# A fused attention, routing and MLP kernel on one core: a new order of the attention, fewer key transfers, one bank for the slots, earlier gathers

## The chip, the core and the metric

The kernel runs on one core of one Trainium2 chip. The time is the device time of one execution in microseconds (us). The core's engines work side by side, each through its own list of instructions in program order: PE multiplies matrices (its weight loads, PEld, overlap), DVE and ACT and POOL work on vectors, SP issues transfers. Matmul results stand in PSUM, eight banks; the other data in SBUF. An instruction that waits holds up all that stand behind it on its engine.

## What is computed

Three stages in a row on 4 batches of 768 tokens, width 384.

```python
# 1: linear attention, 8 heads of 48, complex decay a (|a| clipped at 0.999)
for t in range(768):
    S_re, S_im = ar * S_re - ai * S_im + k_t (x) v_t, ar * S_im + ai * S_re
    y[t] = q_t @ S_re
# 2: mixture of experts: a token with x @ w_skip > 0 goes to its best of 8 experts
e = argmax(x @ w_gate); out = x + prob[e] * relu(x @ w1[e]) @ w2[e]   # w1: 384 x 1024
# 3: dense MLP
h = x @ w_in; out = (h * sigmoid(h)) @ w_out                          # w_in: 384 x 2048
```

## The kernel before

**Attention.** The 768 tokens are six chunks of 128, and the batches two pairs; the pair of a chunk and a batch pair is a step, 12 in all (s = 0 to 11). For each step the kernel loads a, k, q and v; takes the logarithm of the magnitude and the angle of a (`clip`, `ln`, `exp`, `z`, `sq`, `ln1p`, `atan`); sums both over the chunk by matmuls with triangular matrices (L309: `lsc`, `lpu`, `lpy`, `run` for the log sums, `rpy`, `rpu`, `rpx`, `rtp`, `run` for the angles); takes exponentials, sine and cosine; and multiplies k and q by them (`kc`, `qc` with the cosine, `ksn`, `qsn` with the sine, all L243, into the tiles `o`). Steps 0 and 1 do this in two halves, one batch each (`CUTS`).

The result `o`, with real and imaginary parts in two tiles C and S, must be laid out anew, channel by channel, as `KQ`. Transfers from SBUF to SBUF do this (L446, one per row of `PIECES`, five for each of C and S and half). PE then transposes the keys (`tp`, L472), takes scores (`sc`, L482), masks them (`P`, on DVE), multiplies by the values (`py`, L500, and by the state, L504), forms the update of the state (`pu`, L515), and turns the result (`yT`) back into rows of tokens (`px`, L532), which are copied (`xr`) and stored (L541).

**Routing.** After each chunk the logits are taken (`lg` in the table, `pl` on PE, L575), flipped by a small matmul (L584) and copied (`lgo`, L590). From them DVE makes the best expert, the rank of each token within its expert, and a one-hot matrix; matmuls (L835) turn these into slots, 256 tokens for each expert: token numbers (`slots[0]`, read at L858 to L866) and gates (`slots[1]`). The last chunk has its own part (`r1...`), the rest is `r0...`. Each kind of slot has a PSUM tile of its own.

**Order.** Attention and routing are not scheduled by the compiler: `PLACE` gives each piece of each step a position (two values for the two halves), `TAIL` each piece of the routing, and `at` sorts them. Each engine's list is in that order. `ENG` says which engine does a piece (V is DVE, G is POOL, A is ACT). The queues are in the same order: SP issues loads, key transfers and stores one behind the other, POOL the indirect transfers.

**Experts.** Of each expert's 256 tokens POOL gathers two tiles of 128 rows (L989); PE turns them (`pt`, L1001; `xh` is ACT's rounded copy, L1059), multiplies up (`ph`, L925 and L935), ReLU, down (`py`, L935); DVE applies the gates (L1045), POOL scatters the rows back (L1049). A scatter waits for the one before it, since they write the same buffer. Where gathered tokens are late, small matmuls on ones keep PE going (L982). The order comes here from times: `start(e)` is 16.35 x e - 6, and `at(start(e & 6) - 28 + ...)` places the gathers of experts 4 to 7, both experts of a pair at the same time.

**Dense MLP.** Six groups of 512 tokens; POOL gathers the first groups' rows back (`xr`, L1339), PE turns them (`pt`, L1347), multiplies up, ACT and DVE do the SiLU, PE multiplies down, and the result is stored.

Of the kernel before, what the change touches and what calls it, by code (L numbers as in the profile page):

```python
# [8 lines left out]
F32 = mybir.dt.float32  # L9
# [15 lines left out]
W = 2 * H * D  # L25
# [4 lines left out]
DP = 64  # L30
# [9 lines left out]
    "ldA": (0, 5, 10, 40, 85, 48, 103, 261, 306, 336, 397, 494),  # L40
    "clip": ((1, 2), (15, 14), 20, 61, 153, 159, 278, 281, 368, 386, 451, 542),
# [6 lines left out]
    "expc": ((28, 27), (106, 87), 113, 182, 242, 307, 356, 427, 486, 530, 595, 659),  # L48
    "stt2": ((37, 38), (109, 97), 118, 190, 250, 321, 375, 450, 491, 540, 622, 685),
    "cumL": ((39, 42), (115, 104), 138, 208, 266, 343, 391, 453, 525, 554, 625, 689),  # L50
    "expE": ((47, 50), (124, 112), 170, 228, 273, 347, 416, 485, 550, 565, 645, 723),
    "expI": ((53, 83), (123, 120), 162, 220, 280, 350, 414, 478, 537, 567, 653, 714),
    "atan": ((12, 18), (56, 66), 68, 147, 209, 268, 324, 392, 454, 511, 590, 691),
    "cumA": ((16, 34), (59, 72), 93, 176, 234, 288, 362, 426, 499, 583, 656, 732),
    "tn1": ((17, 44), (75, 77), 114, 194, 253, 309, 372, 429, 506, 586, 662, 743),
    "wrap": ((29, 45), (89, 91), 126, 198, 254, 313, 380, 434, 517, 592, 663, 746),
    "car": (67, 111, 141, 236, 272, 326, 418, 484, 526, 599, 0, 0),
    "carl": (73, 116, 142, 247, 312, 328, 439, 497, 552, 606, 0, 0),
    "abs": ((33, 65), (125, 102), 149, 248, 297, 319, 398, 441, 524, 597, 679, 761),
    "sin": ((78, 82), (144, 133), 201, 256, 333, 365, 448, 507, 557, 639, 702, 762),  # L60
    "cos": ((62, 69), (129, 139), 193, 252, 341, 371, 436, 508, 564, 627, 680, 778),
    "ldK": (19, 35, 130, 187, 279, 299, 389, 474, 513, 580, 665, 700),
# [6 lines left out]
    "ksn": ((88, 107), (154, 184), 206, 270, 335, 423, 463, 546, 626, 670, 720, 770),  # L69
    "qsn": ((80, 95), (155, 177), 219, 269, 360, 405, 498, 527, 609, 649, 706, 782),  # L70
    "dmaC": ((100, 128), (164, 213), 257, 295, 366, 417, 496, 573, 650, 696, 763, 804),
    "dmaS": ((101, 110), (178, 207), 239, 285, 385, 440, 509, 566, 652, 697, 750, 792),
    "ldV": (76, 71, 55, 339, 340, 455, 492, 549, 655, 614, 767, 755),
# [31 lines left out]
    "flip": (0, 323, 0, 443, 0, 581, 0, 671, 0, 803, 0, 839),  # L105
    "lgb": (0, 344, 0, 462, 0, 632, 0, 677, 0, 805, 0, 841),
    "lgo": (0, 352, 0, 465, 0, 637, 0, 682, 0, 811, 0, 842),
}
TAIL = {
# [41 lines left out]
def consts(tc, k):  # L151
# [36 lines left out]
    (0, 48, 2, 0, 3, 0, 0),  # L188
    (1, 48, 2, 0, 3, 3, 0),
    (96, 32, 1, 0, 2, 6, 0),  # L190
    (96, 16, 1, 2, 1, 6, 32),
    (112, 16, 1, 2, 1, 7, 32),
)

# [1573 lines left out]
```

## Time and profile before

| what | us |
|---|---|
| three runs | 780.03, 777.7, 779.22 |
| median | 779.22 |
| profiled execution | 778.55 |
| its span (first to last instruction) | 776.8 |
| PE busy | 744.7 (96%), 5499 matmuls |
| DVE busy | 535.4 (69%) |
| ACT busy | 438.2 (56%) |
| POOL busy | 207.4 (27%) |
| mean granted clock of PE | 0.993 of full speed |

The span is 1.75 us shorter than the execution. The attention lasts to about 218 us in the trace, the experts to about 362, the dense MLP to the end. The busy share is a mean over these stages; where PE is idle, and for what it waits, stands in the rows below.

### The profile page before, as it was taken

Reading aid. Unit: us, or ns where it says so; the run is one execution under the profiler, and the core shown is the slowest. Engines: PE = TensorE matmul, PEld = TensorE weight load, DVE = VectorE, ACT = ScalarE, POOL = GpSimd, SP = SyncE. Lnnn points to the kernel's source line nnn. Section 1 sums busy time; section 2 is a strip of 40 time slices with the busy share of each in tenths; the row PEclk is TensorE's granted clock in tenths of the full one; section 3 lists DMA queues with packets and bytes.
Section 4 is the critical chain, followed back from the end, with each engine's and each line's share of the span. In section 5 each row is a group of like instructions: output and inputs, shape, how many; then the busy total and the mean of one; then the engine's idle time right before and its main releaser. Section 6 shows DMA issues by size and latency. Waiting matters only on the chain.

```text
span 776.8 us, 13952 instructions
## 1 busy us (share of the span) xinstructions
PE 744.7 (96%) x5499; PEld 686.8 (88%) x5499; DVE 535.4 (69%) x957; ACT 438.2 (56%) x718; POOL 207.4 (27%) x193
## 2 busy tenths in 40 slices
PE   2799999999999999999999999999999999999995
PEld 2799999998889999999999998988888888888885
DVE  6899889999755867669898333654565656556544
ACT  7899889955435545455676212344555455555543
POOL 4478567123523122423300036810000000000000
PEclk9899999999999999999999999999999999999999
DMA  8567786577838965656760011001000101101001
GB/s 344 166 194 222 267 267 227 164 225 227 276 110 277 304 240 165 248 194 225 228 213 35 1 41 41 1 31 42 12 29 14 42 1 41 41 1 42 1 1 45
DMA packets 31530, 101.87 MB, mean 131 GB/s; under 512 B 4960, under 2 KB 13536, under 8 KB 31456
## 3 DMA queue, kind: packets, MB, share of 16 engines
q1 hardware_dynamic: 26128, 88.05, 34.7%
q0 software_dynamic: 3072, 9.44, 3.3%
q10 hardware_dynamic: 2256, 3.41, 1.4%
q8 instruction: 45, 0.74, 0.4%
q14 instruction: 29, 0.24, 0.1%
HBM read 69.27 MB, written 12.58 MB: 105 GB/s over the span
## 4 chain that ended last, share of the span: by engine, by line
PE 81%; DMA 7%; ACT 4%; DVE 3%; issue 2%; POOL 2%; SPq 1%; another core or an unknown queue 0%; POOLq 0%; DVEq 0%; ACTq 0%
PE ph L935 29%; PE py L935 24%; PE pd L935 6%; PE sc L482 5%; DMA xbuf<-xg,sidx 3%; PE run L309 3%; PE pu L515 2%; PE py L500 2%; PE py L504 2%; PE tp L472 1%; PE ph L925 1%; DMA KQ<-o 1%; PE px L532 1%; DMA xg<-xbuf,gidx 1%; PE pt L1347 1%
## 5 line engine op out<-in xcount | busy, mean ns | idle before, releaser
L935 PE MATMUL ph<-cxh,wh 128*128 128x512 f32 x288 | 113.6, 394 | 0.0
L935 PE MATMUL ph<-cxl,wh 128*128 128x512 f32 x288 | 112.8, 392 | 0.0
L935 PE MATMUL ph<-cxh,wl 128*128 128x512 f32 x288 | 112.6, 391 | 0.0
L1212 DVE TENSOR_TENSOR gl<-g,gh 128x512 fp32r<-128x512 f32 x64 | 44.3, 692 | 88.7 <-ACT gh L1211 45.2
L1210 ACT ACTIVATE g<-ph 128x512 f32<-128x512 f32 x64 | 38.1, 596 | 49.1 <-PE ph L935 48.9
L935 PEld LDWEIGHTS ph<-cxl,wh 128*128 128x128 f32 x288 | 54.0, 188 | 11.6
L935 PEld LDWEIGHTS ph<-cxh,wl 128*128 128x128 f32 x288 | 54.1, 188 | 9.2
L935 PEld LDWEIGHTS ph<-cxh,wh 128*128 128x128 f32 x288 | 54.2, 188 | 9.0
L1232 ACT CAST tz<-twd 128x256 fp32r<-128x256 f32 x96 | 36.6, 408 | 42.5 <-DVE twd L1224 42.5
L1018 DVE TENSOR_TENSOR wl<-raw,wh 128x1536 fp32r<-128x1536 f32 x28 | 48.7, 1758 | 10.7 <-ACT wh L916 10.7
L482 PE MATMUL sc<-KQ 96*128 96x128 f32 x384 | 52.7, 285 | 0.5 <-DMA KQ<-o 0.4
L482 PEld LDWEIGHTS sc<-KQ 96*128 96x128 f32 x384 | 47.8, 197 | 2.7 <-issue 1.4
L935 PE MATMUL ph<-xh,wh 128*128 128x256 f32 x168 | 47.8, 285 | 0.0
L935 PE MATMUL ph<-xl,wh 128*128 128x256 f32 x168 | 47.5, 283 | 0.0
L935 PE MATMUL ph<-xh,wl 128*128 128x256 f32 x168 | 47.5, 283 | 0.0
L916 ACT CAST wh<-raw 128x1536 fp32r<-128x1536 f32 x28 | 40.7, 1478 | 9.0 <-DMA raw<-in_w_dram 7.4
L935 PE MATMUL py<-wh,gl 128*128 128x384 f32 x128 | 43.2, 338 | 0.0
L935 PE MATMUL py<-wh,gh 128*128 128x384 f32 x128 | 43.1, 337 | 0.0
L935 PE MATMUL py<-wl,gh 128*128 128x384 f32 x128 | 43.0, 336 | 0.0
L1049 POOL DMA_INDIRECT xbuf<-xg,sidx x16 | 19.7, 1233 | 86.2 <-DVE xg L1045 24.1
L935 PE MATMUL py<-wh,hh 128*128 128x384 f32 x120 | 40.9, 341 | 0.0
L1211 ACT CAST gh<-g 128x512 fp32r<-128x512 f32 x64 | 39.7, 621 | 2.0
(373 smaller groups left out, 2118.5 us busy)
## 6 DMA issues: line engine op xcount, KB each, us to landing
raw<-in_w_dram SPq DMA_DIRECT2D x30, 768.0 KB
KQ<-o SPq DMA_DIRECT2D x40, 290.2 KB
kq<-in_kq_dram SPq DMA_DIRECT2D x12, 768.0 KB
a<-in_a_dram SPq DMA_DIRECT2D x10, 768.0 KB
raw<-in_w_in_dram SPq DMA_DIRECT2D x8, 768.0 KB
raw<-in_w_out_dram SPq DMA_DIRECT2D x8, 768.0 KB
v<-in_v_dram SPq DMA_DIRECT2D x12, 384.0 KB
xbuf<-xr SPq DMA_DIRECT2D x24, 192.0 KB
```

What stands on the lines that cost most here:

```text
L309: nc.tensor.matmul(p[:, i if bank is None else bank, g * CH:g * CH + CH], a[:, n * CH:n * CH + CH], tri, start=first and g == 0, stop=last ...
L482: nc.tensor.matmul(sc[:, j, :], key(4 * g + j), t.KQ[0:96, 4 * g + j, b, 1, 0:CH], start=True, stop=True)
L500: nc.tensor.matmul(py[64 * i:64 * i + 64, j, :], t.v[:, v0 + h * D:v0 + h * D + DP], u.P[:, h, :], start=True, stop=first)
L504: nc.tensor.matmul(py[64 * i:64 * i + 64, j, :], state[0:96, s0 + h * D:s0 + h * D + DP], t.KQ[0:96, h, b, 1, 0:CH], start=False, stop=True)
L916: nc.scalar.copy(hi, src)
L935: nc.tensor.matmul(out, a, x, start=first and n == 0, stop=last and n == len(pairs) - 1)
L1018: nc.vector.tensor_tensor(u.w[i][1], u.raw[i], u.w[i][0].bitcast(F32), ALU.subtract)
L1049: nc.gpsimd.indirect_dma_start(out=k.x, out_offset=bass.IndirectOffsetOnAxis(ap=k.sidx[:, c:c + 1], axis=0), in_=u.xg[i], in_offset=None)
L1210: nc.scalar.activation(a, u.ph[f], AF.Silu)
L1211: nc.scalar.copy(u.gh[f], a)
L1212: tt(u.gl[f], a, u.gh[f].bitcast(F32), ALU.subtract)
L1232: nc.scalar.copy(h, u.x[:, n])
```

## The change

There are six edits. The numbers of `PLACE`, `TAIL` and `ENG` are new, so attention and routing run in another order and some pieces on another engine. The rows of `PIECES` for the last 16 channels of heads 6 and 7 are interleaved, so three transfers take the place of five. The load of `a` for step 0 comes in four pieces, a half of the tokens' columns each, real and imaginary part, in place of two. The last chunk's rows of the second batch go through the bank `tp`, the other ones through `px`. Both kinds of slots lie in one bank of the tag `pu`; before they had one of `pu` and one of `tp`. The gathers of experts 6 and 7 are placed at the time of expert 5's, 16.35 us earlier in the plan; those of 4 and 5 stay.

Of the tables two lines are shown; the rest of the diff is whole.

```diff
--- before.py
+++ after.py
-    "dmaC": ((100, 128), (164, 213), 257, 295, 366, 417, 496, 573, 650, 696, 763, 804),
...
-    "lg": (0, 302, 0, 431, 0, 575, 0, 669, 0, 790, 0, 837),
...
+    "dmaC": ((103, 136), (175, 202), 238, 302, 364, 425, 494, 577, 619, 682, 748, 789),
...
+    "lg": (0, 308, 0, 446, 0, 588, 0, 663, 0, 805, 0, 835),
...
@@ -188,8 +188,8 @@
     (0, 48, 2, 0, 3, 0, 0),
     (1, 48, 2, 0, 3, 3, 0),
     (96, 32, 1, 0, 2, 6, 0),
-    (96, 16, 1, 2, 1, 6, 32),
-    (112, 16, 1, 2, 1, 7, 32),
+    (96, 16, 2, 2, 1, 6, 32),
+    (97, 16, 2, 2, 1, 7, 32),
 )
 
 
@@ -267,8 +267,9 @@
                 x = pool.tile([128, 2, W], F32, name=n, tag=tag)
                 src = (k.in_a if n == "a" else k.in_kq)[s]
                 if n == "a" and s in CUTS:
-                    for i in range(2):
-                        nc.sync.dma_start(x[:, i], src[:, i])
+                    for sl in CUTS[s] if s == 0 else (slice(0, W),):
+                        for i in range(2):
+                            nc.sync.dma_start(x[:, i, sl], src[:, i, sl])
                 else:
                     nc.sync.dma_start(x, src)
                 if n == "a":
@@ -442,8 +443,9 @@
                 lazy(t, "KQ", lambda: kq[s % len(kq)])
                 b = batches(sl)
                 o = tile(half)[:, :, b]
-                for p0, n, step, g0, ng, h0, d0 in PIECES:
-                    nc.sync.dma_start(t.KQ[every(2 * d0 + half, n, 2), h0:h0 + ng, b], o[every(p0, n, step), g0:g0 + ng])
+                nc.sync.dma_start(t.KQ[every(half, 48, 2), 0:6, b], o[0:96])
+                nc.sync.dma_start(t.KQ[every(half, 32, 2), 6:8, b], o[96:128, 0:2])
+                nc.sync.dma_start(t.KQ[every(64 + half, 16, 2), 6:8, b], o[96:128, 2:3])
 
             for half, x in enumerate("CS"):
                 each(s, "e" + x, lambda i, sl, half=half: ends(half, sl))
@@ -527,7 +529,7 @@
                 tt(sv, tu, dv, ALU.mult)
 
             def rows():
-                px = u.px = ps.tile([128, 4, 2, DP], F32, name="px", tag="px")
+                px = u.px = ps.tile([128, 4, 2, DP], F32, name="px", tag="tp" if last and b else "px")
                 for j in range(4):
                     nc.tensor.transpose(px[:, j].rearrange("p a d -> p (a d)"), t.yT[:, 2 * bp + b, j, :], k.ident)
 
@@ -606,9 +608,10 @@
         end = NSTEP - 1
 
         k.slots = []
-        for tag in ("pu", "tp"):
+        k.bank = None
+        for i in range(2):
             s = Ctx()
-            s.tag, s.tile, s.n = tag, None, 0
+            s.i, s.tile, s.n = i, None, 0
             k.slots.append(s)
 
         def fetch():
@@ -828,7 +831,9 @@
     def fill(g, b, slots):
         m = b.shape[2] * 16
         if slots.tile is None:
-            slots.tile = ps.tile([128, 2, m], F32, name="slots", tag=slots.tag)
+            if k.bank is None:
+                k.bank = ps.tile([128, 2, 2, 48], F32, name="slots", tag="pu")
+            slots.tile = k.bank[:, slots.i, :, 0:m]
         for j in range(4):
             x = b[:, 4 * g + j].rearrange("p a b -> p (a b)")
             i = slots.n - (NT - n if prev else 0)
@@ -1090,7 +1095,7 @@
                 at(8.6 + 1.7 * i, scatter, i)
             return
         for i in range(2):
-            at(2 * e + i - 20 if e < 4 else start(e & 6) - 28 + 2 * (e % 2) + i, gather, i)
+            at(2 * e + i - 20 if e < 4 else start(2 + e // 2) - 28 + 2 * (e % 2) + i, gather, i)
             s = T - 7.7 + 0.1 * i
             at(s, turn, i)
             at(s + 0.4, turn_hi, i)
```

The same places in the instruction lists, before and after. On SP, the key transfers of step 0 (`KQ_143`; `o` with a number is the tile C or S) before:

```order
L273 DMA a<-in_a_dram 128x1536
L446 DMA KQ_143<-o_286 48x3x258 x2
L446 DMA KQ_143<-o_286 32x2x258
L446 DMA KQ_143<-o_286 16x258 x2
L446 DMA KQ_143<-o_280 48x3x258 x2
L446 DMA KQ_143<-o_280 32x2x258
L446 DMA KQ_143<-o_280 16x258 x2
L273 DMA a<-in_a_dram 128x1536
L446 DMA KQ_143<-o_280 48x3x258 x2
```

and after:

```order
L274 DMA a<-in_a_dram 128x1536
L446 DMA KQ_143<-o_320 48x6x258
L447 DMA KQ_143<-o_320 32x2x258
L448 DMA KQ_143<-o_320 16x2x258
L446 DMA KQ_143<-o_309 48x6x258
L447 DMA KQ_143<-o_309 32x2x258
L448 DMA KQ_143<-o_309 16x2x258
L274 DMA a<-in_a_dram 128x1536
```

For each batch six transfers are issued in place of ten.

On PE, the end of the attention from the last up-projection or slot work to the last rows (`ph` on `KQ` is the up-projection of expert 0's first tokens, `pl` the logits and their flip, `px` the rows); the slots' small matmuls are left out. Before:

```order
L925 MATMUL ph_2657<-KQ_143,raw 128x128 x6
L575 MATMUL pl<-yT,w_86 32x128 x16
...
L584 MATMUL pl_2693<-ident,sl 128x128
L532 MATMUL px<-ident,yT 128x128 x4
L925 MATMUL ph_2657<-KQ_143,raw 128x128 x6
L532 MATMUL px<-ident,yT 128x128 x4
...
L532 MATMUL px<-ident,yT 128x128 x4
L925 MATMUL ph_2747<-KQ_143,raw 128x128 x6
L532 MATMUL px<-ident,yT 128x128 x4
```

and after:

```order
L651 MATMUL tp_2596<-ident,xg_67 128x128 x3
L577 MATMUL pl<-yT,w_86 32x128 x16
L534 MATMUL px<-ident,yT 128x128 x4
L586 MATMUL pl_2631<-ident,sl 128x128
...
L534 MATMUL px<-ident,yT 128x128 x4
L930 MATMUL ph_2664<-KQ_143,raw 128x128 x6
L534 MATMUL px<-ident,yT 128x128 x4
```

The logits stand ahead of the first half of the up-projection, and three groups of rows follow them in place of four.

On POOL, the gathers (`xg<-xbuf`, or `xr<-xbuf` for the dense MLP) and scatters (`xbuf<-xg`) before:

```order
L989 DMA xg<-xbuf,gidx 128x384 x7
L1049 DMA xbuf<-xg_67,sidx 3200x384
L1049 DMA xbuf<-xg,sidx 3200x384 x3
L989 DMA xg<-xbuf,gidx 128x384 x4
L1049 DMA xbuf<-xg,sidx 3200x384 x4
L989 DMA xg<-xbuf,gidx 128x384 x4
L1049 DMA xbuf<-xg,sidx 3200x384 x4
L1339 DMA xr<-xbuf,order 128x384 x4
```

and after:

```order
L994 DMA xg<-xbuf,gidx 128x384 x7
L1054 DMA xbuf<-xg_67,sidx 3200x384
L1054 DMA xbuf<-xg,sidx 3200x384 x3
L994 DMA xg<-xbuf,gidx 128x384 x4
L1054 DMA xbuf<-xg,sidx 3200x384 x2
L994 DMA xg<-xbuf,gidx 128x384 x4
L1054 DMA xbuf<-xg,sidx 3200x384 x6
L1344 DMA xr<-xbuf,order 128x384 x4
```

The gathers of experts 6 and 7 (the second `x4`) stand behind two scatters, those of expert 2, and no longer behind four.

In the first part of DVE's list, up to the first product of the keys (`o<-kq,cs`), there stand 31 operations on a half step (128x384) where there were 21.

## Rows read from the trace of the kernel before

**Rows 1.** Busy time by stretch, us: stretch, length, then each engine, PEclk, DMA, GB/s
```profile
20.00:50.00 30.00, 26.20 (x200) 25.12 (x201) 27.81 (x49) 27.74 (x46) 20.24 (x20) 0.89 0.63 176
50.00:100.00 50.00, 49.74 (x552) 46.83 (x551) 44.22 (x67) 46.27 (x69) 33.67 (x25) 1.00 0.77 243
...
400.00:500.00 100.00, 100.00 (x515) 90.76 (x514) 53.75 (x68) 35.86 (x58) 33.57 (x26) 1.00 0.12 39
```

**Rows 2.** What PE waited for, us: total, times, longest
```profile
PE rpy L309 <- ACT a L403: 8.4, 1, 8.4
...
PE ph L925 <- ACT xh L1059: 1.6, 1, 1.6
PE pt L1347 <- DMA xr<-xbuf,order: 1.4, 1, 1.4
PE py L500 <- ACT yT L247: 1.2, 1, 1.2
PE lpy L309 <- DVE s L361: 1.0, 1, 1.0
PE sc L482 <- DMA KQ<-o: 0.4, 1, 0.4
```

**Rows 3.** The stretch from 30 to 40 us, columns as in the first group
```profile
30.00:40.00 10.00, 9.02 (x69) 8.44 (x68) 9.46 (x17) 8.75 (x16) 6.25 (x7) 0.70 0.69 183
```

**Rows 4.** Timeline to 36 us: start us, us, engine, line, operation, shapes, count [idle]
```profile
14.02 2.93 PE L309 MATMUL lsc<-tri_half,s 128*128 128x128 f32 x12 [2.72 <-DVE s L361]
...
32.91 3.31 PE L482 MATMUL sc<-KQ 96*128 96x128 f32 x15
...
15.41 0.56 DVE L406 TENSOR_TENSOR sn<-rpu,sn 128x384 f32<-128x384 f32 x1
...
20.82 0.56 DVE L243 TENSOR_TENSOR o<-kq,cs 128x384 f32<-128x384 f32 x1 [0.21 <-ACT cs L412]
...
23.78 7.23 SPq L446 DMA_DIRECT2D KQ<-o  x10
```

**Rows 5.** Chain that ended last, at the start and near 195: start us, us, what
```profile
0.82 3.21 DMA a<-in_a_dram
...
194.77 3.85 DMA KQ<-o
```

**Rows 6.** Timeline from 198 to 236 us, of PE, then DVE, then POOL
```profile
198.62 1.35 PE L482 MATMUL sc<-KQ 96*128 96x128 f32 x10 [0.43 <-DMA KQ<-o]
...
218.19 1.08 PE L575 MATMUL pl<-yT,w 128*32 128x128 f32 x32
...
225.16 0.60 PE L532 MATMUL px<-ident,yT 128*128 128x128 f32 x4
...
229.55 0.37 PE L835 MATMUL slots<-r1bg,r1hot 128*128 128x48 bf16 x8
...
233.27 0.94 PE L982 MATMUL ph<-ones 128*128 128x128 bf16 x14
235.77 1.49 PE L925 MATMUL ph<-xh,raw 128*128 128x128 f32 x11 [1.56 <-ACT xh L1059]
...
226.58 0.17 DVE L866 TENSOR_TENSOR gidx<-base,slots 128x16 uint32<-128x16 f32 x1
...
229.52 0.97 POOL L989 DMA_INDIRECT xg<-xbuf,gidx  x1 [14.32 <-DVE r1bg L790]
```

**Rows 7.** Timeline of gathers and scatters on POOL; then expert 5's gates on DVE
```profile
314.99 2.24 POOL L989 DMA_INDIRECT xg<-xbuf,gidx  x1 [5.08 <-DMA xbuf<-xg,sidx]
...
330.56 0.99 POOL L1049 DMA_INDIRECT xbuf<-xg,sidx  x1 [6.18 <-DMA xg<-xbuf,gidx]
...
348.08 0.96 POOL L1049 DMA_INDIRECT xbuf<-xg,sidx  x1 [6.05 <-DMA xbuf<-xg,sidx]
351.41 1.07 POOL L1339 DMA_INDIRECT xr<-xbuf,order  x1 [2.37 <-DMA xbuf<-xg,sidx]
...
335.64 1.13 DVE L1045 SCALAR_TENSOR_TENSOR xg<-py,gate,xg 128x384 f32<-128x384 f32 x2
```

More of the change, by code (lines that the diff above doesn't have):

```diff
@@ L39 @@
 PLACE = {
-    "ldA": (0, 5, 10, 40, 85, 48, 103, 261, 306, 336, 397, 494),
-    "clip": ((1, 2), (15, 14), 20, 61, 153, 159, 278, 281, 368, 386, 451, 542),
[6 rows of a table removed]
[L48 to L62, printed above, removed]
[6 rows of a table removed]
-    "ksn": ((88, 107), (154, 184), 206, 270, 335, 423, 463, 546, 626, 670, 720, 770),
-    "qsn": ((80, 95), (155, 177), 219, 269, 360, 405, 498, 527, 609, 649, 706, 782),
@@ L71 @@
-    "dmaC": ((100, 128), (164, 213), 257, 295, 366, 417, 496, 573, 650, 696, 763, 804),
-    "dmaS": ((101, 110), (178, 207), 239, 285, 385, 440, 509, 566, 652, 697, 750, 792),
-    "ldV": (76, 71, 55, 339, 340, 455, 492, 549, 655, 614, 767, 755),
[31 rows of a table removed]
-    "flip": (0, 323, 0, 443, 0, 581, 0, 671, 0, 803, 0, 839),
-    "lgb": (0, 344, 0, 462, 0, 632, 0, 677, 0, 805, 0, 841),
-    "lgo": (0, 352, 0, 465, 0, 637, 0, 682, 0, 811, 0, 842),
+    "ldA": (0, 1, 2, 41, 49, 92, 126, 246, 319, 355, 478, 416),
@@ new lines @@
+    "clip": ((3, 4), (11, 10), 33, 73, 160, 190, 221, 339, 357, 440, 524, 476),
[6 rows of a table added]
+    "expc": ((44, 37), (71, 69), 118, 178, 244, 313, 336, 423, 503, 512, 610, 668),
+    "stt2": ((48, 50), (81, 85), 140, 184, 262, 324, 370, 451, 511, 537, 631, 697),
+    "cumL": ((52, 53), (90, 86), 144, 199, 273, 332, 378, 458, 516, 554, 639, 706),
+    "expE": ((58, 72), (117, 110), 159, 215, 280, 341, 395, 480, 523, 563, 650, 711),
+    "expI": ((60, 59), (108, 119), 155, 222, 285, 343, 399, 471, 521, 569, 655, 715),
@@ new lines @@
+    "atan": ((25, 27), (34, 32), 89, 131, 210, 277, 327, 386, 470, 549, 643, 647),
+    "cumA": ((28, 35), (65, 40), 111, 173, 248, 293, 356, 424, 489, 584, 661, 720),
+    "tn1": ((36, 39), (70, 42), 116, 183, 252, 305, 371, 431, 500, 586, 671, 722),
+    "wrap": ((46, 43), (75, 47), 125, 185, 255, 306, 374, 443, 505, 591, 675, 733),
+    "car": (56, 100, 171, 216, 292, 337, 389, 462, 513, 603, 0, 0),
+    "carl": (77, 128, 188, 249, 318, 338, 396, 490, 561, 615, 0, 0),
+    "abs": ((62, 64), (114, 51), 187, 236, 303, 359, 428, 454, 525, 614, 687, 749),
@@ new lines @@
+    "sin": ((80, 93), (129, 133), 194, 267, 330, 375, 457, 498, 572, 638, 693, 780),
+    "cos": ((76, 88), (123, 137), 196, 257, 321, 388, 439, 464, 547, 628, 694, 753),
+    "ldK": (30, 79, 138, 207, 270, 317, 413, 463, 522, 593, 616, 721),
[6 rows of a table added]
+    "ksn": ((97, 102), (154, 170), 209, 274, 369, 381, 484, 527, 602, 667, 708, 786),
+    "qsn": ((96, 105), (139, 150), 201, 272, 334, 400, 482, 510, 585, 646, 699, 782),
+    "dmaC": ((103, 136), (175, 202), 238, 302, 364, 425, 494, 577, 619, 682, 748, 789),
@@ L108 @@
+    "dmaS": ((104, 135), (180, 182), 234, 295, 384, 437, 518, 579, 630, 689, 766, 794),
+    "ldV": (91, 13, 45, 312, 309, 459, 496, 559, 564, 627, 744, 795),
[31 rows of a table added]
+    "flip": (0, 316, 0, 461, 0, 622, 0, 673, 0, 811, 0, 836),
+    "lgb": (0, 361, 0, 466, 0, 640, 0, 676, 0, 828, 0, 839),
+    "lgo": (0, 372, 0, 472, 0, 649, 0, 678, 0, 830, 0, 841),
 }
 TAIL = {
[7 rows of a table removed]
[7 rows of a table added]
 }
 ENG = {
-    "z": "VGVVVGGVGGVV", "qe": "VGGVGVVVGVVG", "ks": "GVVGVGGGVVVV", "kc": "GVVGGGVVVGVG", "qc":
-    "VGVGVGGGGVGV", "ksn": "VGGGGVGGGGGV", "qsn": "VGVGGVVGVVGV", "P00": "VVVVVVVVVVVV", "kn00":
[3 rows of a table removed]
@@ L124 @@
-    "VVVAAAAAAAVA", "abs": "VVVAAAAVAAVA", "carl": "GGVVGGGGGVGG",
+    "z": "VVVGVGGVGGGV", "qe": "VVGVGVGGGVGG", "ks": "GVGGGVGVGVGV", "kc": "VVVVVGVVGGGV", "qc":
+    "VGGVGVGGVVVV", "ksn": "VVGGGGVGGGGG", "qsn": "VGGVGVGGGVGV", "P00": "VVVVVVVVVVVV", "kn00":
[3 rows of a table added]
+    "VVAAAAAAAAAA", "abs": "VVAAAAVAAVAA", "carl": "VVGGGGGGGVGG",
 }
```

104 rows, old and new, of tables (ENG, PLACE, TAIL) are left out of this document.

## The prediction

> **What bounds the kernel now.** I read the page's first lines, then the busy time by stretch, then what TensorE (PE) waited for, then the timelines around those waits. The busy table [rows 1] shows PE full from 50 us on (49.74 of 50, later 100 of 100); PE is idle 776.8 - 744.7 = 32.1 us in all, and DVE and ACT are never the fuller engine after 50 us. So a change of order on the other engines pays only where PE waits. The list of PE's waits [rows 2] says where that is: five matmuls of the running sums (rpy the first, lpy the last), 18 us together, all before 33 us; py 1.2 and sc 0.4 near 190 to 199; ph on xh 1.6 near 235; pt on xr 1.4 near 362. What stands behind the last matmul (the last store) is in no part of the change. To the idle time one cost comes that no wait shows: in the ten microseconds from 30 the granted clock is 0.70 [rows 3], that is 6 of them at 1.2 GHz and not 2.4 (10 x 0.3 / 0.5), after PE had worked only on and off. From about 36 to 190 us nothing waits, so a moment won at the start is kept to the end, and one lost is too.
>
> The sum is made on the profiled execution: 776.8 us of span and 1.75 outside it, 778.55. The median of the three runs is 779.22, 0.67 above; that is added at the end.
>
> **Start (before 40 us), 0.4 us gained, from -2.5 to +2.5.** Before, the chain is: load lands at 4.0 [rows 5], clip, ln, exp, matmul of the log sums (lsc) at 14.02, exponentials and cosine on ACT, the first key product (o<-kq,cs) on DVE at 20.82, the transfers of the keys from 23.78, first scores at 32.91 [rows 4].
> - The load of step 0 in four pieces. The first two pieces are half as long, so the clip could start a little before 4.0. It is not in the sum for itself: of the 3.21 us to the landing [rows 5] no row shows how much goes with the size, and the next point covers it.
> - The new order puts more in front of the first key product on DVE: 31 half-step operations instead of 21 and about as many long ones. One is 0.47 us (0.56 in its row, pipelined) [rows 4], so 10 x 0.47 = 4.7, less about 1.9 for long ones that left (the long square goes to ACT), 2.8 us more. lsc now stands behind the angles of three halves (three atan on ACT, three times 1.5 us of matmuls, three wraps on DVE): I work it out at 18.9 instead of 14.02. From lsc to the first product were 6.8 us, so it comes at about 25.7, and its transfers can go at 26.5, 2.7 later than 23.78.
> - Against it: the transfers of batch 0 were ten issues in 7.23 us [rows 4], 0.72 each; now they are six. 6 x 0.62 (the median issue of before in this stretch) = 3.7. The last leaves at 30.2 and lands about 2 us after its issue, as before (last issue 31.0, scores 32.91): 32.2. Batch 1 was complete at about 40.5 and is now at 36 to 37, and step 1 follows as much sooner. The matmuls of the log sums that stood in front of the first score are the same.
> - So first scores at 32.5 instead of 32.9: 0.4. If all that the shorter issue gives (3.5) were hidden and only the later product counted, 2.7 would be lost; if the shorter issues of both batches count in full and the clock comes back sooner, 2.5 are won. I take the value near the middle since the two rows almost cancel.
>
> At this place the Trainium skill, page "DMA: Bandwidth & Descriptors", section "Rules for kernel authors", says to coalesce small transfers, and its section on the anatomy of one DMA gives about 2.0 us fixed for each. By that, four transfers fewer are worth 8 us in a row, and the two additional loads of step 0 cost up to 4. The rows speak for less: an issue is 0.72 us, and the scores start 1.9 us behind the last of ten issues, not ten times 2.0 behind the first. By the page the start would gain 4; by the rows 0.4.
>
> **36 to 190 us, 0.** DVE, ACT and POOL are filled to 44, 46 and 34 of 50 [rows 1] and what moved between them is 1.5 us less on DVE in all. PE has no wait here that could go. New waits are possible; the list shows the old order had nearly none in 1.5 hundred microseconds, so the bounds are 0 to +2 us lost.
>
> **190 to 200 us, 1.0 gained, from -2 to +1.85.** py on yT 1.25, sc on KQ 0.6. The chain of waits shows the second: SP's queue of issues, then a transfer of 3.85 us that ends when sc starts [rows 5, 6]. With three issues instead of five for each of C and S, 4 x 0.6 = 2.4 us leave the queue, and the wait of 0.6 with them. In the new order the keys of step 10 are transferred 34 places ahead of their first use, not 13. For py the yT copy has other work before it; I take a third of it as gained, 0.4. The other end: two steps (1 and 4) now have 6 places only between transfer and use, and a miss there costs up to 2.
>
> **200 to 236 us, 1.9 gained, from 0.5 to 3.5.** From the last logits (pl, 218.19) to the first expert matmul with gathered tokens (235.77) are 17.58 us; the last px is at 225.16, the first gather at 229.52, and small filler matmuls (two rows of 14, as the one at 233.27) stand around a wait and in front of the last one of 1.56 [rows 6]. From the first filler, 3.8 us before the gathered tokens' ph, on nothing is of use; with the waits of px, 0.7, that makes 4.5 us. The four px take turns with one bank: each waits for the copy of the one before it. Now two banks take turns, one px stands before the logits, and only three follow. Also, half an up-projection that stood before the logits now stands behind them, so the chain starts earlier while PE has the same work. Worked out: pl 1.05, three px 0.5 each, small ones 0.9, half up 0.75, waits 0.5: last px ends 4.7 after the logits (before 7.6). The chain of the routing on DVE (from logits to slot numbers 8.6, in the old run) then binds: gather at 9.5 after the logits instead of 11.3, up at 15.6 instead of 17.6; 1.9 of the 4.5 go. Low end: the routing chain is the bound and is not shorter, 0.5; high end: one store less at the end too, 3.5.
>
> The slots now share one bank. The last gate matmuls of before stood 3 us behind the reads of the token slots [rows 6], so an order between them costs PE nothing; if it did, a read of 0.17 us, twice, 0.4 at most. The Trainium skill, page "PSUM — Partial Sum Buffer", section "PSUM bank collisions raise a hardware error", says to guard by bank and not by address, so that two users of one bank go one after the other. This speaks against the shared bank, by the same 0.4: the sum would be 1.5 in place of 1.9.
>
> **361 us, 1.2 gained, from 0 to 1.4.** pt waits 1.39 for xr. On POOL the gathers of experts 6 and 7 were issued from 314.99 and the next scatter waited for their landing until 330.56, four scatters followed, one after another's landing, to 348.08, then the xr gathers at 351.41 [rows 7]. The gates for expert 5 were applied at 335.64 [rows 7], so the scatters were late by the queue, not by DVE. With those gathers two scatters sooner, expert 5's scatters can go from 336.7 and 344.7 (8 us between two as before), xr at about 348, 3.4 sooner: PE itself arrives 3.3 sooner by the other terms, so that nearly all of the 1.39 goes and hardly more could: 1.2. None of it if scatters of expert 3 are held up by the gathers as those of expert 4 were.
>
> **Sum.** 0.4 + 0 + 1.0 + 1.9 + 1.2 = 4.5. 778.55 - 4.5 = 774.05, plus 0.67 = 774.7.
>
> **Rivals.**
> - Hidden anyway. PE is full between 36 and 361 but for 6 us, and the routing chain near 220 is the same list of DVE operations; then only the wait at 361 goes. For it: the 100 of 100 of [rows 1]. Against it: the waits of px and the filler are no work. 779.22 - 1.4 = 777.8.
> - Slower: late keys and a slow PE. Place: 24 to 40 us on PE. DVE is busy 27.81 of the 30 us from 20 [rows 1], and the first key product is worked out at 5 us later. If the transfers' issues are not what binds, scores start 3.0 later (26.5 plus the 9.1 from first issue to first score of before = 35.6, and 0.3 for the more products that DVE does in step 0). PE then idles longer and works at the lower clock longer; before, this was 6 us, and once more 6 at half speed cost 3.0. 6.0 lost against 4.1 won later: 779.22 + 1.9 = 781.1. It decides from a first score later than 37 us on. For it: clock 0.70 in [rows 3]. Against it: the 3.5 us of issues saved.
> - All waits after 190 go: 1.85 + 4.5 + 1.4 = 7.75, and 1.5 at the start: 779.22 - 9.25 = 770.0. For it: three of the four waits are of queues that get shorter. Against it: the routing chain on DVE keeps its length.
>
> **How the numbers follow.** Forecast 0.53 (its own range 771.5 to 777.3), hidden 0.20, late keys 0.13, all waits 0.14. 0.3%, 2.3 us, is about what a measurement of this kernel can tell from no change: faster is below 776.9. Faster: 0.14 + 0.49 of the forecast + 0.04 of the hidden one = 0.67. Slower: nearly all of late keys, and the bad end of the unpriced waits, 0.12. Same 0.21. The range goes from half a microsecond below the best rival to just short of the slow one, 769.5 to 781.0, with about 0.1 left out at each side.
>
> **What would show it.** First scores between 32 and 34 us with six issues before them (above 37: late keys). PE's waits without sc on KQ near 198 and without pt on xr. From last logits to first gathered ph 15 to 16 us; at 17.5 that step was wrong. No new wait above 1 us between 36 and 190; three or more would make the whole wrong, and so would a lower clock after 40 us.

## The result, and the profile after

The changed kernel is slower. Its median is 786.05 us (781.34 to 789.62, 17 runs), that of the kernel before, run on the same chip, 780.27 us; the ratio is 1.0065, 95% interval [1.0046, 1.0085], so about 5 us. The forecast was 774.7, and the range ended at 781.0. The profiled execution took 785.52 us with a span of 783.8, against 778.55 and 776.8 before: 7.0 us apart. The comparisons below are of profiles where a place is named and of timed ratios where a price is.

First the busy time by stretch in the changed kernel (columns as in [rows 1]: stretch, length, then PE, PEld, DVE, ACT, POOL, granted clock, DMA share, GB/s).

```profile
20.00:50.00 30.00, 22.73 (x185) 21.80 (x186) 25.89 (x50) 27.37 (x45) 14.97 (x19) 0.84 0.74 205
30.00:40.00 10.00, 9.17 (x70) 8.87 (x70) 9.42 (x19) 9.93 (x18) 3.97 (x4) 0.84 0.70 188
50.00:100.00 50.00, 48.57 (x527) 46.38 (x525) 46.02 (x68) 46.01 (x67) 33.39 (x25) 0.97 0.76 231
65.00:70.00 5.00, 4.24 (x28) 4.27 (x29) 3.75 (x7) 3.91 (x6) 2.04 (x2) 0.73 0.87 323
210.00:215.00 5.00, 4.88 (x67) 4.33 (x68) 3.69 (x15) 0.44 (x2) 2.05 (x2) 0.66 1.00 315
400.00:500.00 100.00, 100.00 (x512) 90.68 (x511) 58.56 (x73) 37.71 (x59) 27.77 (x22) 1.00 0.16 54
```

The row from 50 to 100 us answers to the 49.74 at clock 1.00 of [rows 1]: PE is idle 1.4 us there and the clock is 0.97, and the rows of five microseconds show where: 0.73 from 65 to 70, and once more 0.66 from 210 to 215. From 400 us on nothing has changed, as before. At the start the clock is higher than before in the ten microseconds of [rows 3] (0.84, not 0.70), but lower over the thirty from 20 us on (0.84, not 0.89), and PE is busy there 22.73 us and not 26.20.

What PE waited for in the changed kernel (total us, times, longest), against [rows 2]:

```profile
PE rpy L310 <- ACT a L404: 12.9, 1, 12.9
PE lpu L310 <- DVE s L362: 5.0, 1, 5.0
PE lsc L310 <- DVE s L362: 2.5, 1, 2.5
PE pl L577 <- DVE xr L249: 2.4, 1, 2.4
PE sc L484 <- DMA KQ<-o: 1.9, 2, 1.4
PE tp L474 <- issue: 1.5, 1, 1.5
PE py L940 <- DVE hl L935: 1.1, 2, 0.6
PE tp L474 <- DMA xbuf<-xr: 0.9, 1, 0.9
PE run L310 <- DVE s L362: 0.8, 1, 0.8
PE pt L1006 <- DMA xg<-xbuf,gidx: 0.8, 1, 0.8
PE tp L474 <- DMA KQ<-o: 0.6, 1, 0.6
```

The waits that the prediction spoke of (py on yT, ph on xh, pt on xr) are gone. In their place stand a wait of 2.4 for a copy on DVE and a row of waits for keys: sc and tp on KQ, and tp on "issue", a wait whose end the profile does not show; load_behind, below, shows that it is for keys.

Where the time went is read by counting PE's work: at equal work done, how far does the changed kernel's profile lag behind the one of before? It leads by 0.35 us at 40 us, lags by 4.4 at 72 and 6.8 at 171, 5.6 at 203, 8.2 at 229, 6.7 at 246, 9.0 at 280, and 7.2 from 372 us to the end (times of before up to 171, of after from 203 on). So 7.15 us are lost between 40 and 171, the stretch in which the forecast had a zero.

The start, in the changed kernel's timeline (start us, us, engine, line, operation, count [idle]), as in [rows 4]:

```profile
12.89 1.62 PE L310 MATMUL rpy<-tri_turn,a 128*128 128x128 f32 x6 [12.89 <-ACT a L404]
...
19.18 2.64 PE L310 MATMUL lsc<-tri_half,s 128*128 128x128 f32 x12 [2.51 <-DVE s L362]
...
34.39 1.87 PE L484 MATMUL sc<-KQ 96*128 96x128 f32 x15
...
27.51 0.77 SPq L446 DMA_DIRECT2D KQ<-o  x1
...
31.45 0.60 SPq L448 DMA_DIRECT2D KQ<-o  x1
...
26.41 1.03 DVE L243 TENSOR_TENSOR o<-kq,cs 128x384 f32<-128x384 f32 x2
```

The first matmul is 4.5 us later than before (12.89, not 8.40), the log sums 5.2, the first product 5.6, the first score 1.5. Yet no wait stands in front of that score: PE does the running sums of later steps first, and so has lost nothing at 40 us.

The chain that ended last, near 60 us (start us, us, what):

```profile
57.93 1.61 SPq L448
...
59.65 5.97 DMA KQ<-o
65.62 0.14 issue
65.76 1.13 PE sc L484 x8
```

The last three transfers of step 2's keys are issued from 59.65 and land 6 us later; PE had nothing to do for 1.37 us, and then worked at the lower clock (the 0.73 above). Five such places lie between 40 and 171: at step 0's second batch tp waits 1.47 until 42.9; at step 2 sc waits 1.37 until 65.8, with 1.7 more from the clock (0.73 of five microseconds and 0.93 of the next five); at step 5 sc waits 0.50 until 115.0, at step 6 tp 0.62 until 133.7, and at step 8 tp 0.93 until 169.5. Together that is 6.6 of the 7.15. The last of them stands in the list as a wait for a store (xbuf<-xr), but it is for keys too: those issued from 162.26 on landed at 169.33.

Around 206 us, on DVE, POOL and PE:

```profile
206.26 3.33 DVE L853 TENSOR_TENSOR r1oh<-r0pre,short 1x1 bf16<-1x1 bf16 x1
209.52 0.54 DVE L249 COPY xr<-px 128x384 f32<-128x384 f32 x1
...
206.15 3.44 POOL L633 TENSOR_TENSOR wl<-o,wh 128x1536 fp32r<-128x1536 f32 x1
...
210.12 1.46 PE L577 MATMUL pl<-yT,w 128*32 128x128 f32 x32 [2.42 <-DVE xr L249]
```

One DVE operation on a single number took 3.33 us. It started 0.11 behind POOL's operation and ended with it (209.59 both). Behind it in DVE's queue stood the copy that the logits' matmuls wait for.

The end of attention, answering to [rows 6]:

```profile
225.72 1.20 PE L577 MATMUL pl<-yT,w 128*32 128x128 f32 x32
...
229.78 0.60 PE L534 MATMUL px<-ident,yT 128*128 128x128 f32 x4
...
241.32 0.55 PE L1006 MATMUL pt<-ident,xg 128*128 128x128 f32 x3 [0.78 <-DMA xg<-xbuf,gidx]
241.70 0.94 PE L987 MATMUL ph<-ones 128*128 128x128 bf16 x14
242.48 2.90 PE L930 MATMUL ph<-xh,raw 128*128 128x128 f32 x24
...
234.19 0.17 DVE L871 TENSOR_TENSOR gidx<-base,slots 128x16 uint32<-128x16 f32 x1
...
238.03 0.99 POOL L994 DMA_INDIRECT xg<-xbuf,gidx  x1 [19.01 <-DVE em L879]
```

From the last logits to the last px are 4.1 us (7.0 before), but the slot numbers come 8.5 behind the logits, as before (8.4), and the gather 12.3 behind them (11.3 before). The first up-projection on gathered tokens is 16.8 behind the logits, 0.8 less than the 17.6 of [rows 6]. In between PE has half an up-projection more to do than before, and it waits 0.8 where it waited 2.4 (four waits of 0.14, 0.29, 0.41 and 1.56): by the count of work 1.5 us are won between 229 and 246.

Last POOL near 350 us, answering to [rows 7]:

```profile
351.67 0.96 POOL L1054 DMA_INDIRECT xbuf<-xg,sidx  x1 [5.42 <-DMA xbuf<-xg,sidx]
357.93 0.98 POOL L1344 DMA_INDIRECT xr<-xbuf,order  x1 [5.30 <-PE pt L1006]
```

The gathers xr no longer wait for a scatter but for PE's pt, and PE's wait for xr is gone; the lag falls by 1.7 us there.

### The profile page after: what moved, and what is told of

It reads as the page before. It is cut to its first block, busy times and chain, and to the rows that moved or that the text cites. A ratio compares the mean times of both kernels' runs of the same rounds, so it can differ in the third digit from the quotient of the medians.

```text
span 783.8 us, 13830 instructions
## 1 busy us (share of the span) xinstructions
PE 744.9 (95%) x5499; PEld 687.0 (88%) x5499; DVE 535.8 (68%) x963; ACT 442.0 (56%) x717; POOL 209.3 (27%) x192
## 4 chain that ended last, share of the span: by engine, by line
PE 82%; DMA 6%; DVE 4%; issue 3%; SPq 2%; POOL 2%; ACT 1%; DVEq 0%; POOLq 0%; ACTq 0%
PE ph L940 32%; PE py L940 26%; PE pd L940 6%; PE sc L484 4%; PE run L310 2%; DMA KQ<-o 2%; PE pu L517 2%; PE py L502 2%; PE tp L474 1%; PE py L506 1%; DMA raw<-in_w_dram 1%; SPq L448 1%; PE pt L1352 1%; PE px L534 1%; POOL kq L243 1%
## 5 line engine op out<-in xcount | busy, mean ns | idle before, releaser
L1215 ACT ACTIVATE g<-ph 128x512 f32<-128x512 f32 x64 | 38.2, 597 | 49.3 <-PE ph L940 49.1
L940 PE MATMUL py<-wh,hl 128*128 128x384 f32 x120 | 40.6, 338 | 1.1 <-DVE hl L935 1.1
L1054 POOL DMA_INDIRECT xbuf<-xg,sidx x16 | 17.2, 1075 | 90.4 <-DMA xbuf<-xg,sidx 42.9
```

Source lines behind the costliest of these rows:

```text
L940: nc.tensor.matmul(out, a, x, start=first and n == 0, stop=last and n == len(pairs) - 1)
L1054: nc.gpsimd.indirect_dma_start(out=k.x, out_offset=bass.IndirectOffsetOnAxis(ap=k.sidx[:, c:c + 1], axis=0), in_=u.xg[i], in_offset=None)
L1215: nc.scalar.activation(a, u.ph[f], AF.Silu)
```

## The experiments

The first question was which part of the change costs. My theory was the new order (the tables PLACE, TAIL and ENG); the rival was the transfers, loads and bank.

**old_order**: the changed kernel with the tables of before.

```diff
-    "ldA": (0, 1, 2, 41, 49, 92, 126, 246, 319, 355, 478, 416),
+    "ldA": (0, 5, 10, 40, 85, 48, 103, 261, 306, 336, 397, 494),
...
-    "e1": 685, "x1": 688, "x3": 691, "fw": 728, "sa0": 729, "x2": 731, "e2": 732, "e3": 738, "g2": 739, "x4":
+    "e1": 692, "x1": 705, "e2": 711, "e3": 713, "g2": 724, "x2": 728, "e5": 739, "fw": 740, "g3": 751, "g1":
...
```

> All edits of the change except the three tables: the attention and routing run in the order of before, with three key transfers, the four loads of step 0, one bank for the slots, the other bank for the last rows and the earlier gathers. Theory (the new order is at fault, it puts waits on PE between 36 and 216 us): none of the waits of the changed kernel at 41 (1.5), 64 (1.4), 110 to 170 (2.4) and 208 us (2.4) are there, sc on KQ near 198 (0.6) and pt on xr (1.4) are gone too: about 2 us below before, ratio to before 0.996 to 0.999. Rival (the edits besides the order are at fault, above all the last rows and slots sharing banks): as slow as the changed kernel, ratio 1.005 to 1.008.

Measured: 779.53 us, ratio to before 1.0000 [0.9978, 1.0022]. So the three transfers, the four loads, the shared bank and the other gathers cost nothing together, and give nothing that can be told either. Its profile has no wait on "issue" and 0.5 us on KQ. It has px waiting 1.2 for DVE near 182 and sc 1.6 on the values v near 197, which the profile of the kernel before has not. The first is not the edits' doing: it stands in gathers_only too, whose one edit acts some 120 us later, so the waits of one order differ from one execution to the next.

**new_order_only**: the changed tables and the bank that they need, with five transfers, two loads and the gathers of before.

```diff
-            at(2 * e + i - 20 if e < 4 else start(2 + e // 2) - 28 + 2 * (e % 2) + i, gather, i)
+            at(2 * e + i - 20 if e < 4 else start(e & 6) - 28 + 2 * (e % 2) + i, gather, i)
...
-                nc.sync.dma_start(t.KQ[every(half, 48, 2), 0:6, b], o[0:96])
+                for p0, n, step, g0, ng, h0, d0 in PIECES:
```

> The changed kernel with the five key transfers, the two loads of step 0 and the old place of the gathers; the new tables and the banks stay. Theory (the order is at fault, the transfers help it): slower than the changed kernel by the xr wait (1.4 us) and by later keys (ten issues for six in the first two steps), ratio to before 1.008 to 1.016. Rival (the four small loads and the three transfers cost the time): the two waits at 41 and 64 us go and the first clip of the second half comes near 4.5 and not 5.3 us: ratio 1.000 to 1.004.

Measured: 787.65 us, ratio 1.0108 [1.0064, 1.0152]. Since the banks are in old_order too, the order is the loss. That the other edits take some of it back (1.0108 against 1.0065) is likely but not shown, since the two intervals overlap.

The next three take single places out of the new order. "Early" and "behind" are moves of one number each.

**start_op_early**: the two operations of L852 and L853 before POOL's long one.

```diff
-    "e5": 793,
+    "e5": 760,
```

> The changed kernel with one thing moved: the two small DVE operations that start the last chunk's count (bf16, the second on one element) stand some ten operations sooner, beside no long POOL operation. In the changed kernel the second took 3.33 us, from 206.26 to 209.59, and a POOL operation of 3.44 us ran from 206.15 to 209.59. Theory (DVE was held until POOL's operation ended): it takes 0.15 to 0.2 us, PE's wait of pl for the copy xr (2.4) is below 0.4, the granted clock of the stretch from 210 to 215 is 1.00 (it was 0.66), and the time falls by 3 to 4 us against the changed kernel: ratio to before 1.001 to 1.003. Rival (the operation itself is slow, or waits for its operand): it takes 3 us at the new place too and the time does not fall.

Measured: 782.09 us, 1.0047 [1.0015, 1.0080]. L853 takes 0.15 us at 193.7, and the wait of pl is gone:

```profile
L853 DVE TENSOR_TENSOR r1oh<-r0pre,short x1: 150/150/150, 193.7 to 193.7; 1x1 bf16<-1x1 bf16 x1
```

**load_behind**: the load of step 6 behind the key transfers of step 0's second batch, in front of which it waited on SP until 34.14 us for a buffer that PE still read.

```diff
-    "ldA": (0, 1, 2, 41, 49, 92, 126, 246, 319, 355, 478, 416),
+    "ldA": (0, 1, 2, 41, 49, 92, 136.5, 246, 319, 355, 478, 416),
```

> The changed kernel with one load of step 6 moved on SP from in front of the second batch's key transfers of step 0 to behind them. It waited for PE until 34.14 us while the product to be sent was done at 32. Theory (the load held SP's list): those six transfers issue from 32.0 instead of 34.6, the wait of tp at 41 us (1.5) is below 0.3, and the time falls by 1 to 2 us. Rival (the transfers wait for the products or for PE's use of the buffer): issue not before 34, the wait stays above 1.

Measured: 783.68 us, 1.0052 [1.0020, 1.0085]. The six transfers issue from 32.23, not 34.58, and the wait on "issue" is gone; 4.8 us on KQ (sc 3.3, tp 1.5) and 2.0 of pl remain.

**both_moved**: both numbers.

> The changed kernel with both mends: the two small DVE operations sooner, and the load of step 6 behind the key transfers. Theory (they cost 2.4 us of wait with some clock, and 1.5 us): the waits pl on xr and tp near 41 us are both gone, the time is 1 to 2 us below either mend alone, ratio to before 1.000 to 1.003; what is left are waits of tp and sc for key transfers between 36 and 170 us, 3 us or more in all. Rival (the time of the new order is set by something else, and the mends only move it): no better than one mend, ratio above 1.004.

Measured: 780.47 us, 1.0028 [1.0000, 1.0057]. By the ratios the first move gives back 0.18 percentage points, the second 0.13, both together 0.37, that is 2.9 us of the 5.1. Neither move alone can be told from no gain by its time: 1.0047 and 1.0052 lie in the interval of the changed kernel, [1.0046, 1.0085]. 1.0028 lies outside it, though the two intervals still overlap. With both, these waits are the largest in its profile behind the start:

```profile
PE sc L484 <- DMA KQ<-o: 3.4, 4, 1.6
PE pt L1006 <- DMA xg<-xbuf,gidx: 0.8, 1, 0.8
PE run L310 <- DVE s L362: 0.8, 2, 0.5
PE tp L474 <- DMA KQ<-o: 0.6, 1, 0.6
```

What is left on this list is mostly waits for keys. But this execution took 778.39 us, no more than the kernel before: by the count of work it lags 3.4 us at 171, 0.6 at 246 and 1.7 at 280, and 0.0 from 364 on. So what the change gives behind 171 us just pays, in this execution, for what the waits for keys cost before.

**start_op_late**: is it POOL's operation that holds DVE's small one, or its place? In the kernel before, where L848 takes 0.15 us, the two operations are moved beside POOL's.

```diff
-    "e5": 739,
+    "e5": 820.5,
```

> The kernel before with one thing moved: its two small bf16 DVE operations for the last chunk's count (0.15 us each at 187.9) stand behind the first mask of step 11, where two long POOL operations run, 208.35 to 215.2. Theory (DVE is held until POOL's operation ends): the first lasts until about 211.8 and the second 3 us more or until POOL's next ends, the masks behind them come 2 to 5 us late, PE waits that long for them, and the time rises by 2 to 6 us, ratio 1.003 to 1.008. Rival (no such hold, 3.33 us had another reason): 0.15 to 0.5 us each, ratio 0.999 to 1.001.

Measured: 784.36 us, 1.0063 [1.0037, 1.0088]: one number of the old order makes it as slow as the change did. In its timeline (DVE, POOL, then PE):

```profile
207.93 0.69 DVE L486 TENSOR_TENSOR P<-sc,tri 128x512 f32<-128x512 f32 x1 [3.02 <-PE sc L482]
208.53 4.75 DVE L847 COPY r1oh<-r0pre 128x8 bf16<-128x8 bf16 x1
213.32 0.15 DVE L848 TENSOR_TENSOR r1oh<-r0pre,short 1x1 bf16<-1x1 bf16 x1
...
206.42 6.81 POOL L630 TENSOR_TENSOR wl<-o,wh 128x1536 fp32r<-128x1536 f32 x2
...
214.12 2.08 PE L482 MATMUL sc<-KQ 96*128 96x128 f32 x8 [4.21 <-DVE P L486]
```

The copy of eight numbers starts beside the first of POOL's two operations, which ends at 209.86, and lasts until the second one ends (213.23). The masking P, which reads PSUM and one SBUF tensor, ran beside POOL in its usual 0.69. The hold is shown in both orders.

**three_and_gathers** and **gathers_only**: edits that the prediction credited, done alone in the kernel before: the three transfers with the gathers of experts 6 and 7, and the gathers alone.

```diff
-            at(2 * e + i - 20 if e < 4 else start(e & 6) - 28 + 2 * (e % 2) + i, gather, i)
+            at(2 * e + i - 20 if e < 4 else start(2 + e // 2) - 28 + 2 * (e % 2) + i, gather, i)
```

> The kernel before with two edits alone: three key transfers for five, and the gathers of experts 6 and 7 earlier. Order, loads and banks are those of before. Theory: xr no longer waits (1.4), sc on KQ near 198 is gone (0.6), the keys of the first steps come a little sooner: 2 us below before, ratio 0.996 to 0.998. Rival (what the old order gains by these is taken by something that the two edits start, as a later expert waiting): ratio 0.999 to 1.002.

> The kernel before with the gathers of experts 6 and 7 earlier and nothing else. Theory: the wait of pt for xr goes from 1.4 to below 0.2 and the time falls by 1.2 to 1.5 us, ratio 0.998. Rival (the wait goes and comes back as a wait of the experts' own gathers or scatters): wait gone, ratio 0.9995 to 1.001.

Measured: 778.20 us, 0.9999 [0.9979, 1.0018], and 778.21 us, 0.9989 [0.9961, 1.0017]. In both profiles the wait of pt on xr is gone, and the lag at 364 us is 1.6 to 1.7 less; in the timed runs neither can be told from no change. So no gain of the three transfers is seen in the old order, and the wait of sc on KQ near 197, which they were expected to remove, is 1.4 in the profile of three_and_gathers.

The last three start from both_moved and ask what its remaining 0.28% are.

**early_keys**: the products and transfers of steps 2 and 3 earlier in the sequence (two of the eight lines are shown; the others move eC, qc and dmaS of both steps and ks, qsn, ksn of step 3 in front of them).

```diff
-    "kc": ((82, 95), (158, 176), 227, 276, 340, 409, 460, 534, 580, 666, 723, 776),
+    "kc": ((82, 95), (158, 176), 208.5, 262.5, 340, 409, 460, 534, 580, 666, 723, 776),
...
-    "dmaC": ((103, 136), (175, 202), 238, 302, 364, 425, 494, 577, 619, 682, 748, 789),
+    "dmaC": ((103, 136), (175, 202), 220.5, 278.5, 364, 425, 494, 577, 619, 682, 748, 789),
...
```

> The kernel with both mends (load_behind and start_op_early), with the key products and transfers of steps 2 and 3 put 10 to 25 places sooner. Theory (in the new order transfers stand too close to their first use: 5.7 to 6.2 us from the first of three issues to the landing, and DVE makes step 3's products only at 69 us): the waits of sc on KQ at 64 and 79 us (together about 2.5 us with both mends) go, and the time falls by 1 to 2.5 us from 780.5. Rival (DVE is as full as PE here, so that sooner keys make other work late): the waits come back under other names between 50 and 100 us, and the time is within 0.7 us of 780.5.

Measured: 784.13 us, 1.0071 [1.0043, 1.0098]: 0.43 percentage points, 3.4 us, slower than both_moved, and both expectations missed. The keys did not come sooner: step 2's first transfer was issued at 56.75 us, in both_moved at 55.33. What makes them late is not DVE's place. POOL makes three of the four products of step 2, and it waits for ACT's sine; in early_keys DVE's product (53.55 us) then ran beside POOL's pair:

```profile
51.82 4.35 POOL L243 TENSOR_TENSOR o<-kq,sn 128x768 f32<-128x768 f32 x2 [0.66 <-ACT sn L412]
```

In both_moved that pair began at 51.17 and took 3.60. The wait of step 2's first score at 64 us was 1.51 here and 0.92 there, and here the clock fell behind it. The two stretches of early_keys, and then the one of both_moved:

```profile
60.00:70.00 10.00, 8.49 (x69) 8.11 (x68) 8.87 (x12) 7.40 (x12) 5.49 (x6) 0.81 0.84 262
70.00:80.00 10.00, 10.00 (x85) 9.88 (x85) 6.95 (x10) 7.90 (x13) 4.44 (x4) 0.85 0.51 144
```

```profile
60.00:70.00 10.00, 9.08 (x93) 8.69 (x92) 9.69 (x14) 9.42 (x14) 6.53 (x7) 1.00 0.78 247
```

69 matmuls instead of 93 in the same ten microseconds: of the 3.8 us that early_keys falls behind both_moved from 60 to 80 us, the clock makes 3.4 (10 x 0.19 + 10 x 0.15).

**five_both_moved**: five transfers for three.

```diff
-                nc.sync.dma_start(t.KQ[every(half, 48, 2), 0:6, b], o[0:96])
-                nc.sync.dma_start(t.KQ[every(half, 32, 2), 6:8, b], o[96:128, 0:2])
-                nc.sync.dma_start(t.KQ[every(64 + half, 16, 2), 6:8, b], o[96:128, 2:3])
+                for p0, n, step, g0, ng, h0, d0 in PIECES:
+                    nc.sync.dma_start(t.KQ[every(2 * d0 + half, n, 2), h0:h0 + ng, b], o[every(p0, n, step), g0:g0 + ng])
```

> The kernel with both mends, with five transfers for each half of the keys in place of three. Theory (an issue of the three is longer, so that three save about 1.0 us per half on SP's queue): waits on KQ grow by 1 to 3 us in all, the time rises by 1 to 3 us from 780.5. Rival (landing is set by the transfer, 3.9 to 4 us for five and for three, and the queue has slack): within 0.7 us of 780.5.

Measured: 784.99 us, 1.0080 [1.0054, 1.0106]: 0.52 percentage points, 4.1 us, more than both_moved. In the old order no difference between five and three could be told. Its profile shows one wait of 3.5 for keys, which ends at 50 us, and then the clock at 0.51:

```profile
PE tp L473 <- DMA KQ<-o: 4.8, 4, 3.5
...
50.00:55.00 5.00, 4.85 (x30) 4.33 (x31) 0.68 (x3) 3.63 (x5) 4.92 (x3) 0.51 0.42 114
```

On SP the twenty issues of step 1 stand one behind the other from 41.4 to 56.7 us, where both_moved's twelve are over at 49.3. So the key transfers on SP's queue do bind the new order, and no sign of that was seen in the old one. Whether the issues or the transfers themselves are what counts was not separated.

**two_loads_moved**: the load of step 0 in two pieces.

```diff
-                    for sl in CUTS[s] if s == 0 else (slice(0, W),):
-                        for i in range(2):
+                    for i in range(2):
```

> The kernel with both mends, with the load of step 0 in two pieces instead of four. Theory (four pieces let the first clip start 0.8 us sooner but put the loads of step 1 two issues later): first scores (34.4 us) come 0 to 1 us sooner and the first matmul within 0.7 of 12.4 us; the time is within 1 us of 780.5. Rival (four pieces are what makes the first running sums come as early as they do in the new order): the first matmul is over 1 us later and the time rises by 1 us or more.

Measured: 780.94 us, 1.0021 [0.9990, 1.0051], no difference to both_moved that can be told; the first matmul was at 11.8 us, sooner than with four pieces (12.4). No version that was run is faster than the kernel before by more than can be measured.

## Why the prediction was wrong

**The step that failed is "36 to 190 us, 0".** It was bounded at 0 to 2 us lost, and 7.15 were lost in the profile between 40 and 171 us. The bound came from the old order's list of waits, which shows that PE had nearly none there. That is no property of the stretch but of the order that was taken away: a list of waits of before says nothing of a sequence in which some 850 of 935 places are new. The other sign that I read, the places between a step's last transfer and its first use, misled too: steps 1 and 4, with six places only, did not wait, while steps 0 (second batch), 2, 5, 6 and 8 waited with 12 to 21; in the old order step 2 stood with two and did not wait. What was missing is the time: from the first of a step's last three issues to the landing 6 to 8 us pass. The runs show that the waits are the order's (new_order_only 1.0108, old_order 1.0000), that they are for keys (five_both_moved against both_moved: two more transfers for each of C and S cost 4.1 us), and that the load of step 6 in front of the key transfers is one of them (load_behind). Of the signs named in advance, a lower clock after 40 us came, and two new waits above 1 us with a third of 0.93.

**200 to 236 us, 1.9 gained.** From 203 to 246 us 1.1 were lost. First, the hold of L853 at 206, 2.4 us of waiting and 1.7 of clock 0.66, had no term at all; without it the stretch would have gained. The Trainium skill, page "SBUF — State Buffer", section "Who interferes with whom", states that a DVE instruction with two SBUF inputs, or a copy in a mode that uses both ports, and a GpSimd instruction that reads SBUF exclude each other, and that the later one waits for the whole of the other. The hold of 3.33 us agrees, and so does P, which was not held. The copy of 4.75 us agrees in that it was held, but it outlasted the end of one POOL operation and waited for the next one too. Both operations stand in the sequence by a number (e5 for L853), so their nearness could have been given a price in advance. Second, the routing chain: px does end 3 us sooner behind the logits, as worked out, but the slot numbers took 8.5 us as before, and the gather stood 3.8 behind them on POOL (2.9 before). It came 12.3 behind the logits, where I had 9.5; up came 0.8 sooner, not 1.9. So the low end's condition, "the routing chain is the bound and is not shorter", came; yet PE won 1.5 us there and not 0.5, because it had half an up-projection more to do meanwhile. What turned the term round is the hold.

**Start, 0.4 gained: 0.35 in the profile.** The number came out by luck. The log sums (19.2, forecast 18.9) and the first product (26.4, forecast 25.7) were as worked out, but the first scores came at 34.4, 1.5 later than before, and not at 32.5, 0.4 sooner: the six issues began at 27.5 and took 4.5 us, not 3.7. This cost nothing, because the new order gives PE the sums of later steps in between. No gain of the load in four pieces can be told (two_loads_moved). The fixed cost of each transfer in the Trainium skill ("DMA: Bandwidth & Descriptors", the section on the anatomy of one DMA) is given there for transfers that GpSimd issues, and the ones here are issued by SP; the 4 us that I worked out from it did not come.

**190 to 200 us, 1.0 gained.** The lag falls by 1.2 between 171 and 203, and neither py on yT nor sc on KQ stands there with more than 0.3. Right in size, but the way to it is not shown: with three transfers in the old order sc still waited 1.4 near 197 (three_and_gathers), and the wait of py on yT was 0.3 in gathers_only, whose attention is that of the kernel before. Nor are the keys of step 10 transferred 34 places ahead of their first use; by the table it is 7 (`dmaS` at 766, `sc01` at 773).

**361 us, 1.2 gained.** The lag falls by 1.6 to 1.8 in each of the profiles with the new gathers, a little over the 1.4 that was the upper bound. The way was right, but 0.2% is less than the timed runs can tell (gathers_only 0.9989).

**The rival "late keys and a slow PE"** had the mechanism that decided, at the wrong place and with a condition that did not come: it asked for a first score later than 37 us, and that came at 34.4. Keys were late at step 0's second batch and at steps 2, 5, 6 and 8, each time because transfers that take 6 to 8 us from issue to landing began less than that before PE was free for them.

Not settled: what is left with both moves, 0.28% [0, 0.57]. Its profile has 4.0 us of waits for keys, but is no slower than that of the kernel before, and early_keys, meant to take two of the waits away, did not make the keys sooner. Also not followed is a loss of 2.3 us between 246 and 280 in the changed kernel (py on hl 1.1 of it); with the same code there both_moved shows 1.2, load_behind 0.5 and start_op_early none.

## What to carry to other kernels

Before an order of a full machine is replaced, list for every transfer whose landing PE needs how far ahead of its use it now stands, in microseconds and not in places of the table, and set that against the time from issue to landing; that the old order had no wait is no bound for the new one. Look also at which small DVE operations with SBUF inputs now stand beside a long POOL operation, and what is queued behind them. The same shorter queue gave nothing that could be measured in one order here and 4.1 us in another, so price such an edit in the order in which it will run.

## What the runs showed of the hardware

A copy of eight bf16 numbers for each partition and an operation on one number each lasted until a POOL operation beside them ended, 4.75 and 3.33 us in place of 0.15 to 0.17; the copy through the end of one POOL operation and the whole of the next.

A wait can cost more than its length. Behind waits of 3.5 and 4.2 us the granted clock was 0.51 to 0.54 in the next five microseconds, behind 1.37 and 1.51 it was 0.73 and 0.62, but behind 0.92 and 1.60 in both_moved it stayed at 1.00. The start differs in the same way with the same code: from 20 to 40 us the clock was 0.67 and then 0.84 in the changed kernel, and 1.00 in start_op_early, whose order is the same up to 190. Single runs spread widely (778.1 to 789.1 for start_op_early, 777.4 to 782.0 for old_order, 776.1 to 786.1 for the kernel before beside them); that the clock is the reason is not shown. So one profile can be several microseconds from its kernel's median: that of start_op_early was 778.43 with a median of 782.09, that of load_behind 779.80 with 783.68, that of five_both_moved 780.95 with 784.99.

The third issue of the key transfers, the smallest of the three, held SP 1.6 to 1.7 us at 58 and 61 us, where the first two took 0.5 to 0.6.
